# Where the early work of a fused backward kernel is placed: transposes, late tables and weight-gradient pieces in the first eight steps

## The chip, the cores and the metric

The kernel runs on one core of one Trainium2 chip. The metric is the device time of one execution in microseconds (us), the median of several runs. The core has a matrix engine (TensorE, "PE" in the profile), a vector engine (VectorE, "DVE"), a scalar engine for activations and copies (ScalarE, "ACT"), a general engine (GpSimd, "POOL") and a queue that only issues transfers (SyncE, "SP"). Each works through its own list of instructions, and they meet through semaphores. Matmul results land in PSUM, [...]from which ACT or DVE must copy them before the bank can be used again.

## The reference

A gate mixes two branches, and the kernel returns the mixture and the gradients of all inputs but one:

```python
g = sigmoid((x * gate_w).sum(-1, keepdims=True))
a = irfft2(rfft2(x) * (w_r + 1j * w_i))           # over 2048 x 576
b = (gelu(x @ w_gate) * (x @ w_up)) @ w_down      # 576 -> 4608 -> 576
out = g * a + (1 - g) * b
# and, for grad_out: the gradients of x, w_r, w_i, w_gate, w_up, w_down, gate_w
```

x and grad_out are 2048 x 576 in bf16. In the kernel the Fourier transforms are matmuls with tables of sines and cosines.

## The kernel before

**Tiling.** The 2048 rows are 16 tiles of 128. The 4608 hidden columns are worked on in 18 groups g of 256 (`NG`, `FG`). A group has four steps m, each over four row tiles, so there are 72 steps, numbered pr = 4g + m. A second phase after the 72 steps multiplies stored results with the weights; the change does not touch it.

**A step.** `H_mm` (L378) lists the matmuls: z, the gradient dOT against w_down (L388, L391), and xy, the gate and up products (L395, L402), into two PSUM tiles, called the first and second half here. `H_da` (L409) copies z out on ACT, scaled by 1-g. `H_act` (L415) copies one half of xy out on ACT: part 0 is the square q (L419), part 1 is the plain copies xb and hu (L421, L422). `H_ew1` (L424) is three DVE instructions on q and xb. `H_ew2` (L440) is two sigmoids on ACT (L443, L444) and eight DVE products (L448 to L455), the last of them dHg. Of the working tiles q, s and om there is one buffer each, of xb and hu two. So q of a step cannot be written before the product om (L450) of the step before has read the old q.

**The weight gradients.** `W_units` (L468) lists matmuls over the A, dHu, dHg of one group: four units w (L505), one tail unit (L518), and four units d (L488), which multiply A with the gradient tile dB. They run one group later: those of group 0 in steps 4 to 7, with a rest carried into step 8. Each is evacuated by ACT (L466) and stored by POOL's queue.

**The transforms.** `fft` is a list of some 200 small units, and `want(pr)` says how many are to be done by step pr. In the first steps they are u1 (six matmuls L562, a copy Y on ACT, L567) and u2 (two matmuls L579, a copy ve on ACT, L583, two DVE instructions, a store). `pftile` (L541) gives them their PSUM tile: in group 0 two tiles in turn, named pg and z, and from group 1 on only z, which the step's own z product also uses. The first unit of a step is put between the matmuls of the second half of xy (`between`, L399).

**Other early work.** `titems` (L347) transposes four row tiles in three pieces: matmuls with the identity (L355, L358), then a copy on DVE or ACT (L359). `build_R` (L141) makes four tables: five DVE instructions, and a sine on ACT that is put off until `run_late` (L106). `columns_B` (L158) and `build_B` (L192) make another table in the same way, on DVE and POOL, with a sine in `run_late`. `scale_dB` (L940) multiplies tiles of dB by 1-g on DVE, in place; units d need all 16 scaled, the transposes need them unscaled.

The order on every engine is that in which the Python program calls the instructions; there is no planner that reorders.

Of the kernel before, what the change touches and what calls it, by code (L numbers as in the profile page):

```python
# [20 lines left out]
P, T = 128, 16  # L21
# [207 lines left out]
def kernel(  # L229
# [4 lines left out]
    nc = tc.nc  # L234
# [64 lines left out]
    tb = iotas(nc, res, unit)  # L299
# [109 lines left out]
    def H_da(m, z):  # L409
        da = ewt("da")  # L410
        for t in range(4):
            nc.scalar.activation(da[:, t, :], z[:, t % 2, t // 2, :], ACT.Copy, scale=omg32[:, 4 * m + t:4 * m + t + 1])  # L412
        return da

    def H_act(k, xy, tiles, part):  # L415
        xb, q, hu = tiles
        h = slice(2 * k, 2 * k + 2)
        if part == 0:
            nc.scalar.activation(q[:, h, :], xy[:, :, 0:FG], ACT.Square)  # L419
        else:  # L420
            nc.scalar.copy(xb[:, h, :], xy[:, :, 0:FG])  # L421
            nc.scalar.copy(hu[:, h, :], xy[:, :, FG:2 * FG])  # L422

    def H_ew1(tiles):  # L424
        xb, q, hu = tiles
        s = ewt("s")
        V.tensor_scalar(s[:], q[:], A_GELU, 1.0, op0=ALU.mult, op1=ALU.add)
        V.tensor_tensor(s[:], xb[:], s[:], op=ALU.mult)
        V.tensor_scalar(q[:], q[:], 6.0 * A_GELU * C_GELU, 2.0 * C_GELU, op0=ALU.mult, op1=ALU.add)
        return s  # L430
# [37 lines left out]
    def W_units(g):  # L468
        fsl = slice(g * FG, (g + 1) * FG)
        kt = kept[g]  # L470

        def tl(k, t):
            return kt[t // 4][k][:, t % 4, :]
        dwd_tiles, wp = {}, {}

        def halves(f, us):
            return [(us, lambda: f(0)), (us, lambda: f(1))]

        def wtile(key):
            if key not in wp:  # L480
                wp[key] = pw.tile([P, TPB, FG], F32, tag="wps", name="wps")
            return wp[key]

        def u_dwd(fch, h):
            def f(half):
                wps = wtile(("d", fch, h)).rearrange("p a b -> p (a b)")
                for t in range(8 * half, 8 * half + 8):
                    nc.tensor.matmul(wps[:, :288], lhsT=tl(0, t)[:, fch * P:(fch + 1) * P],  # L488
                                     rhs=dB[:, t, h * 288:(h + 1) * 288], start=(t == 0), stop=(t == T - 1))
                if half == 0:  # L490
                    return
                if h == 0:
                    dwd_tiles[fch] = stage.tile([P, D], BF16, tag="dwd", name="dwd")
                dwd = dwd_tiles[fch]
                wevac(dwd[:, h * 288:(h + 1) * 288], wps[:, :288])
                if h == 1:
                    r0 = g * FG + fch * P
                    wst[0].dma_start(out_6[r0:r0 + P, :], dwd[:])
            return halves(f, 1.0)

        def u_dw(k, ov, c0):
            def f(cc):
                wps = wtile(("w", k, c0))
                for t in range(T):
                    nc.tensor.matmul(wps[:, cc, :], lhsT=xn[:, t, (c0 + cc) * P:(c0 + cc + 1) * P],  # L505
                                     rhs=tl(k, t), start=(t == 0), stop=(t == T - 1))
                if cc == 0:
                    return
                dw = stage.tile([P, TPB, FG], BF16, tag="dw", name="dw")
                wevac(dw[:], wps[:])  # L510
                wst[0].dma_start(ov[:, c0:c0 + TPB, fsl], dw[:])  # L511
            return halves(f, 1.7)

        def tail(half):
            wps = wtile("t")
            for t in range(8 * half, 8 * half + 8):
                for k, r in ((1, LO), (2, HI)):
                    nc.tensor.matmul(wps[r, 0, :], lhsT=xn[:, t, 512:576], rhs=tl(k, t),  # L518
                                     start=(t == 0), stop=(t == T - 1))
            if half == 0:  # L520
                return
            dw = stage.tile([P, FG], BF16, tag="dwt", name="dwt")
            wevac(dw[:], wps[:, 0, :])
            wst[0].dma_start(out_4[512:576, fsl], dw[LO, :])
            wst[0].dma_start(out_5[512:576, fsl], dw[HI, :])
        tl_ = halves(tail, 1.0)
        w = [u_dw(k, ov, c0) for k, ov in ((1, o4v), (2, o5v)) for c0 in range(0, 4, TPB)]
        d = [u_dwd(fch, h) for fch in range(FCH) for h in range(2)]
        if g == 0:
            return [[w[0], tl_], d, [w[1]], [w[2]], w[3]]  # L530
        return [[d[0]], [d[1], d[2], d[3]], [w[0], tl_], [w[1], w[2]], w[3]]


# [347 lines left out]
    build_R(nc, tb, unit, 0)  # L881
    build_R(nc, tb, unit, 4)
    run_late(tb)
    columns_B(nc, tb, res)
    makeB = build_B(nc, tb, unit, res)

    fg = zipped(*fwd_units(xT, scr_x, None)) + zipped(*fwd_units(dOT, scr_g, gs32))
# [17 lines left out]
    mid_at = 4 * T + 10  # L905
    NPR = NT // 2
    LASTP = NG * NPR - 7
    FIRST = (0, 0, 1, 3)
    done = [0]

    def want(pr):

        n0 = FIRST[-1]
        if pr < NPR:
            return FIRST[pr]

        def load(n):

            return n + 0.5 * min(max(n - mid_at, 0), n_mid)
        share = load(n0) + (load(n_slots) - load(n0)) * (pr + 1 - NPR) / (LASTP - NPR)  # L920
        n = n0
        while n < n_slots and load(n + 1) <= share + 1e-9:
            n += 1
        return int(min(n, n_slots) + 1e-9)
# [20 lines left out]
    for g in range(NG):  # L945
        if g == 1:
            pgs.close()
            pw = ps1.enter_context(tc.tile_pool(name="pw", bufs=2, space=PSUM, **kw))
        for m in range(NPR):
            pr = g * NPR + m  # L950
            n = want(pr) - done[0]
            done[0] += n
            hs = [h for u in pend[m] for h in u] if pend else []

            def side_work(us):
                while side and us > 0:
                    us -= side[0][0]
                    side.pop(0)[1]()
            z, xy_full = H_mm(g, m)
            tiles = [ewt(tag) for tag in ("xb", "q", "hu")]  # L960
            xy = xy_full(0)
            da = H_da(m, z)
            H_act(0, xy, tiles, 0)
            flush()
            H_act(0, xy, tiles, 1)
            state = []
            titem = titems(dB, dOT, 4 * m + 8, pgtile, (VC, VC, AC)) if g == 0 and m < 2 else []
            if titem:
                titem.pop(0)()

            def second():
                xy = xy_full(1, titem.pop(0) if titem else fft_next if n else None)
                for part in range(2):
                    H_act(1, xy, tiles, part)
                state.append(H_ew1(tiles))
                side_work(4.4)

            def sigs():
                H_ew2(g, m, tiles, state[0], da)
            if g == 0:  # L980
                second()
                for f in titem:
                    f()
                for _ in range(n - 1):
                    fft_next()
                sigs()
                if m == 0:
                    next(makeB)
                elif m < 3:
                    build_R(nc, tb, unit, 4 * m + 4)  # L990
                else:
                    next(makeB)
            else:
                second()
                at, k = 0.0, min(n, 1)
                spots = (0.0, 1.6, 3.6) if n < 4 else (0.0, 1.0, 2.6, 4.2, 5.0, 5.0)
                for w, f in carry + hs:
                    if k < n and at >= spots[k]:
                        fft_next()
                        k += 1  # L1000
                    if pr == NG * NPR - 1 and at == 0.0:
                        sigs()
                    f()
                    at += w
                while k < n:
                    fft_next()
                    k += 1
                if pr == NPR:
                    run_late(tb)
                if pr < NG * NPR - 1:  # L1010
                    sigs()
            carry = []
            flush(len(stores) - 1)
            if m < 3 and g + 1 < NG:
                load_w(g + 1, m)
            if (g, m) in ((0, 3), (1, 0)):
                scale_dB(T // 2)
            if done[0] == n_slots or (pr >= wgT_from and pr % 2 == 0 and len(wgT_all) < 20):
                load_wgT()
                if done[0] == n_slots:  # L1020
                    load_wgT()
        carry = pend[4] if pend else []
        pend = W_units(g)
# [241 lines left out]
```

## Time and profile before

| what | value |
|---|---|
| median of three runs | 1427.95 us (1427.85 to 1428.72) |
| the profiled execution | 1427.79 us |
| its span in the profile | 1426.0 us |
| busy PE / DVE / ACT / POOL | 1389.1 / 730.4 / 727.0 / 124.5 us |
| chain that ended last, by engine | PE 92%, DVE 3%, ACT 3%, issue 1% |
| PE busy from 20 to 130 us | 90.4 of 110 us |
| PE busy from 130 to 300 us | 170 of 170 us |

The span is the time from the first to the last instruction of the profile; the execution's own time is 1.8 us more. A busy PE is counted from modelled ends of pipelined matmuls, so short gaps can hide in it. All times in the text are counted from the start of the span.

### The profile page before, as it was taken

Reading aid. Unit: us, or ns where it says so; the run is one execution under the profiler, and the core shown is the slowest. Engines: PE = TensorE matmul, PEld = TensorE weight load, DVE = VectorE, ACT = ScalarE, POOL = GpSimd, SP = SyncE. Lnnn points to the kernel's source line nnn. Section 1 sums busy time; section 2 is a strip of 40 time slices with the busy share of each in tenths; the row PEclk is TensorE's granted clock in tenths of the full one; section 3 lists DMA queues with packets and bytes.
Section 4 is the critical chain, followed back from the end, with each engine's and each line's share of the span. In section 5 each row is a group of like instructions: output and inputs, shape, how many; then the busy total and the mean of one; then the engine's idle time right before and its main releaser. Section 6 shows DMA issues by size and latency. Waiting matters only on the chain.

```text
span 1426.0 us, 28214 instructions
## 1 busy us (share of the span) xinstructions
PE 1389.1 (97%) x11431; PEld 1022.3 (72%) x11431; DVE 730.4 (51%) x1395; ACT 727.0 (51%) x1321; POOL 124.5 (9%) x226
## 2 busy tenths in 40 slices
PE   7789999999999999999999999999999999999997
PEld 5456767676667767767777777768777777777776
DVE  6765656555988877775656566551000642212100
ACT  7667777768878788776777777662000000000000
POOL 3000000110101101110010100110000100000000
PEclk9999999999999999999999999999999999999999
DMA  5333433444546655555455564759999998778773
GB/s 179 96 99 113 129 113 109 120 138 124 145 134 171 163 137 149 150 146 141 118 159 157 137 165 128 170 126 248 211 195 203 224 191 168 163 153 168 155 150 77
DMA packets 514655, 214.63 MB, mean 151 GB/s; under 512 B 311418, under 2 KB 508732, under 8 KB 514524
## 3 DMA queue, kind: packets, MB, share of 16 engines
q1 hardware_dynamic: 504988, 192.32, 56.9%
q0 software_dynamic: 7728, 19.49, 4.2%
q8 instruction: 89, 1.46, 0.4%
q10 hardware_dynamic: 1808, 1.02, 0.3%
q14 instruction: 42, 0.34, 0.1%
HBM read 41.05 MB, written 93.84 MB: 95 GB/s over the span
## 4 chain that ended last, share of the span: by engine, by line
PE 92%; DVE 3%; ACT 3%; issue 1%; DMA 0%; POOL 0%; SPq 0%; POOLq 0%; DVEq 0%; ACTq 0%
PE acc L1110 29%; PE wps L505 17%; PE xy L402 16%; PE wps L488 10%; PE z L388 8%; PE wps L518 2%; PE xy L395 2%; PE pf L562 2%; PE z L391 1%; PE pf L833 1%; PE pf L761 1%; PE pf L835 1%; PE pf L672 1%; PE pf L579 0%; ACT s L444 0%
## 5 line engine op out<-in xcount | busy, mean ns | idle before, releaser
L1110 PEld LDWEIGHTS <-pin 128*128 128x128 bf16 x3456 | 338.0, 98 | 85.3 <-issue 0.2
L402 PE MATMUL xy<-wgu,xT 128*128 128x512 bf16 x1152 | 271.7, 380 | 0.0
L505 PEld LDWEIGHTS <-xn 128*128 128x128 bf16 x2304 | 224.9, 98 | 39.4 <-issue 1.2
L402 PEld LDWEIGHTS <-xT 128*128 128x128 bf16 x1152 | 106.0, 98 | 136.9 <-issue 30.9
L1127 ACT COPY bo<-acc 128x288 f32<-128x288 f32 x32 | 12.8, 400 | 305.0 <-PE acc L1110 305.0
L448 DVE TENSOR_TENSOR xb<-xb,s 128x1024 bf16<-128x1024 bf16 x72 | 49.9, 692 | 223.0 <-ACT s L444 222.8
L488 PE MATMUL wps<-dB,A 128*128 128x288 bf16 x1152 | 154.5, 286 | 0.3 <-DVE dB L942 0.3
L1110 PE MATMUL acc<-wgT,pin 128*128 128x288 bf16 x1152 | 143.8, 286 | 0.0
L1110 PE MATMUL acc<-wuT,pin 128*128 128x288 bf16 x1152 | 143.6, 286 | 0.0
L1110 PE MATMUL acc<-wd_all,pin 128*128 128x288 bf16 x1152 | 142.6, 286 | 0.0
L388 PE MATMUL z<-wdT,dOT 128*128 128x256 bf16 x1152 | 137.8, 273 | 3.9 <-ACT Y L567 2.4
L505 PE MATMUL wps<-dHg,xn 128*128 128x256 bf16 x1152 | 136.7, 273 | 0.8 <-DVE dHg L455 0.8
L488 PEld LDWEIGHTS <-A 128*128 128x128 bf16 x1152 | 112.2, 98 | 32.6 <-issue 1.8
L505 PE MATMUL wps<-dHu,xn 128*128 128x256 bf16 x1152 | 135.5, 273 | 0.0
L388 PEld LDWEIGHTS <-dOT 128*128 128x128 bf16 x1152 | 111.2, 98 | 22.4 <-issue 8.4
L419 ACT ACTIVATE q<-xy 128x512 bf16<-128x512 f32 x144 | 87.8, 610 | 63.2 <-DVE om L450 56.5
L412 ACT ACTIVATE da<-z,omg 128x256 bf16<-128x256 f32 x288 | 111.8, 470 | 0.6 <-PE z L391 0.6
L1187 DVE SCALAR_TENSOR_TENSOR f32t<-gwf,dlog,b16t 128x576 f32<-128x576 f32 x16 | 13.1, 817 | 172.5 <-DMA b16t<-dxa_scr 172.5
L511 POOL DMA_DIRECT2D out_dram<-dw x67 | 49.2, 734 | 581.1 <-ACT dw L466 576.4
L422 ACT CAST hu<-xy 128x512 bf16<-128x512 f32 x144 | 89.0, 618 | 0.0
L421 ACT CAST xb<-xy 128x512 bf16<-128x512 f32 x144 | 85.6, 595 | 0.0
L466 ACT CAST dw<-wps 128x512 bf16<-128x512 f32 x72 | 42.2, 586 | 78.0 <-PE wps L505 77.7
(207 smaller groups left out, 1596.6 us busy)
## 6 DMA issues: line engine op xcount, KB each, us to landing
scr<-A SPq DMA_DIRECT2D x72, 256.0 KB, 2.4
scr<-dHg SPq DMA_DIRECT2D x72, 256.0 KB, 2.7
scr<-dHu SPq DMA_DIRECT2D x72, 256.0 KB, 3.0
out_dram<-dw POOLq DMA_DIRECT2D x67, 128.0 KB, 3.0
wd_all<-in_B_w_down_dram SPq DMA_DIRECT2D x3, 1728.0 KB, 14.4
out_dram<-dwd POOLq DMA_DIRECT2D x34, 144.0 KB, 3.3
scr_p<-Vt SPq DMA_DIRECT2D x32, 145.0 KB, 3.4
wgu<-in_B_w_gate_dram SPq DMA_DIRECT2D x18, 256.0 KB, 3.6
```

Source lines behind the costliest of these rows:

```text
L388: nc.tensor.matmul(zo(t), lhsT=dOT[:, ci, t, :], rhs=wdT[:, ci, :], start=(t % 4 < 2 and ci == 0), stop=False)
L402: nc.tensor.matmul(xy[k][:, t % 2, :], lhsT=xT[:, ci, t, :], rhs=wgu[:, ci, :], start=False, stop=(ci == 3))
L412: nc.scalar.activation(da[:, t, :], z[:, t % 2, t // 2, :], ACT.Copy, scale=omg32[:, 4 * m + t:4 * m + t + 1])
L419: nc.scalar.activation(q[:, h, :], xy[:, :, 0:FG], ACT.Square)
L421: nc.scalar.copy(xb[:, h, :], xy[:, :, 0:FG])
L422: nc.scalar.copy(hu[:, h, :], xy[:, :, FG:2 * FG])
L448: V.tensor_tensor(xb[:], xb[:], s[:], op=ALU.mult)
L466: nc.scalar.copy(out, in_)
L488: nc.tensor.matmul(wps[:, :288], lhsT=tl(0, t)[:, fch * P:(fch + 1) * P], rhs=dB[:, t, h * 288:(h + 1) * 288], start=(t == 0), stop=(t == ...
L505: nc.tensor.matmul(wps[:, cc, :], lhsT=xn[:, t, (c0 + cc) * P:(c0 + cc + 1) * P], rhs=tl(k, t), start=(t == 0), stop=(t == T - 1))
L511: wst[0].dma_start(ov[:, c0:c0 + TPB, fsl], dw[:])
L1110: nc.tensor.matmul(acc[:, :288], lhsT=src[:, r, :], rhs=w_of(r)[:, h * 288:(h + 1) * 288], start=(first and r == 0), stop=(last and r == F ...
```

## The change

The three pieces of transposes for row tiles 12 to 15 of the gradient move from step 1 to step 0; those of tiles 8 to 11 stay in step 0. All but the first two of the six pieces now stand ahead of `H_ew1` of that step. In every step the copies of the first half of xy come in the order xb, hu, q in place of q, xb, hu. `columns_B` moves from the head of the kernel to step 5, the two parts of `build_B` from steps 0 and 3 to steps 5 and 6, `build_R` for tables 8 to 11 and 12 to 15 from steps 1 and 2 to steps 5 and 6, and `run_late` for all of these from step 4 to step 6. All 16 tiles of dB are scaled in step 4, between `H_ew1` and `H_ew2`; before, eight were scaled at the end of step 3 and eight at the end of step 4. Of the pieces of group 0's weight gradients, step 5 has three d units and step 6 one d and one w unit; before, step 5 had four d and step 6 one w. The count of transform units by the end of steps 4 to 7 is written out as 6, 10, 14, 17; `want` gave 6, 10, 14, 18 before.

```diff
         if g == 0:
-            return [[w[0], tl_], d, [w[1]], [w[2]], w[3]]
+            return [[w[0], tl_], d[:3], [d[3], w[1]], [w[2]], w[3]]
...
     run_late(tb)
-    columns_B(nc, tb, res)
     makeB = build_B(nc, tb, unit, res)
...
-    FIRST = (0, 0, 1, 3)
+    FIRST = (0, 0, 1, 3, 6, 10, 14, 17)
...
         n0 = FIRST[-1]
-        if pr < NPR:
+        if pr < len(FIRST):
             return FIRST[pr]
...
-        share = load(n0) + (load(n_slots) - load(n0)) * (pr + 1 - NPR) / (LASTP - NPR)
+        share = load(n0) + (load(n_slots) - load(n0)) * (pr + 1 - len(FIRST)) / (LASTP - len(FIRST))
...
             da = H_da(m, z)
+            H_act(0, xy, tiles, 1)
             H_act(0, xy, tiles, 0)
             flush()
-            H_act(0, xy, tiles, 1)
             state = []
-            titem = titems(dB, dOT, 4 * m + 8, pgtile, (VC, VC, AC)) if g == 0 and m < 2 else []
-            if titem:
+            titem = []
+            if pr == 0:
+                titem = titems(dB, dOT, 8, pgtile, (VC, VC, AC)) + titems(dB, dOT, 12, pftile, (VC, VC, AC))
                 titem.pop(0)()
 
             def second():
                 xy = xy_full(1, titem.pop(0) if titem else fft_next if n else None)
                 for part in range(2):
                     H_act(1, xy, tiles, part)
+                while titem:
+                    titem.pop(0)()
                 state.append(H_ew1(tiles))
+                if pr == 4:
+                    scale_dB(T)
+                elif pr == 5:
+                    columns_B(nc, tb, res)
+                    next(makeB)
+                    build_R(nc, tb, unit, 8)
+                elif pr == 6:
+                    next(makeB)
+                    build_R(nc, tb, unit, 12)
                 side_work(4.4)
...
             if g == 0:
                 second()
-                for f in titem:
-                    f()
                 for _ in range(n - 1):
                     fft_next()
                 sigs()
-                if m == 0:
-                    next(makeB)
-                elif m < 3:
-                    build_R(nc, tb, unit, 4 * m + 4)
-                else:
-                    next(makeB)
             else:
...
-                if pr == NPR:
+                if pr == 6:
                     run_late(tb)
...
-            if (g, m) in ((0, 3), (1, 0)):
-                scale_dB(T // 2)
```

## The prediction

> **What bounds the kernel now.** I read three things in order. First the page's busy times by slice: the matrix engine is full everywhere except in the first four slices of 35.65 us.
>
> ```profile
> PE   7789999999999999999999999999999999999997
> DVE  6765656555988877775656566551000642212100
> ```
>
> So a change to the first eight steps can gain only what PE idles there, 19.6 us between 20 and 130 us (90.4 busy of 110); from 130 to 300 us PE is busy 170 of 170. Second, PE's waits between 20 and 170 us, line by line with the releaser:
>
> ```profile
> PE pf L355 <- DVE dOT L359: 5.6, 1, 5.6
> PE pf L562 <- ACT da L412: 4.5, 2, 2.7
> PE pf L579 <- ACT da L412: 3.1, 1, 3.1
> PE pf L562 <- ACT ve L583: 2.6, 3, 1.0
> PE z L388 <- ACT Y L567: 2.4, 3, 0.9
> ```
>
> All of them lie in the stretch concerned. Third, the timeline says what released them. On DVE in steps 1 and 2:
>
> ```profile
> 50.20 0.69 DVE L455 TENSOR_TENSOR dHg<-hu,om 128x1024 bf16<-128x1024 bf16 x1
> 50.80 1.13 DVE L148 SCALAR_TENSOR_TENSOR XR<-kk,scol 128x128 int32<-128x128 f32 x4
> 51.97 0.43 DVE L149 TENSOR_SCALAR XR<-XR 128x512 int32<-128x512 int32 x1
> 52.32 0.42 DVE L427 TENSOR_SCALAR s<-q 128x1024 bf16<-128x1024 bf16 x1
> ...
> 53.56 1.06 ACT L443 ACTIVATE om<-s 128x1024 bf16<-128x1024 bf16 x1 [2.13 <-DVE s L428]
> ```
>
> In group 0 the bound is a loop of ACT and DVE, not PE: two sigmoids (om to the start of DVE's L448, 2.21), eight products (5.19 to the next start), then L427 and L428 (1.24 until om). That is 8.64 us; the table instructions (50.80 to 52.32) make it 10.14, and the sigmoids of steps 1, 2, 3 start at 43.40, 53.56, 63.70. From step 4 the bound passes to PE, with two more losses on the way: the late sines, and the scaling of dB.
>
> ```profile
> 77.07 1.28 ACT L154 ACT_TABLE_LOAD   x1
> 78.37 1.33 ACT L154 ACTIVATE Rt<-XR,pi 128x512 bf16<-128x512 int32 x2
> 79.61 0.49 ACT L222 ACTIVATE oB<-XBi,pi 128x256 f32<-128x256 int32 x1
> 80.12 1.28 ACT L443 ACT_TABLE_LOAD   x1
> 81.41 1.06 ACT L443 ACTIVATE om<-s 128x1024 bf16<-128x1024 bf16 x1
> ```
>
> And on PE, in the next step:
>
> ```profile
> 85.06 0.41 PE L579 MATMUL pf<-Y,Rt 128*128 128x290 bf16 x2 [3.12 <-ACT da L412]
> ```
>
> ACT is busy without a break from 77.07; da comes behind the sigmoids, and the transform unit between the xy matmuls needs the z bank that da empties.
>
> **The Trainium skill.** PSUM — Partial Sum Buffer, "Engine vs sequencer instructions", says that the queues of ScalarE, VectorE and GpSimd are strictly first in, first out. The trace agrees: ACT's q waits 0.81 us in step after step for om (L450) while the ready xb stands behind it. ScalarE: Activation LUTs, "What ACT_TABLE_LOAD costs", gives 1.28 us for a load and 2.66 with a drain. Here the load is 1.28 and the next activation starts 1.30 after it, so I use 1.3. TensorE: Matmul & The Clock Gate, "What's actually happening", says that the array falls to half clock after an idle window of about 3.4 us. The trace agrees: PE idles 5.62 us up to 38.73, and the granted clock from 36 to 42 us is 0.50.
>
> **Part 1, step 0.** Three pieces (24 transposes, three copies) join step 0, and DVE and ACT do their copies ahead of the chain. All run through few PSUM tiles. ACT copies the third piece from 28.64 to 29.3, as now. Piece 4 takes pg: transposes from 29.35, copy on DVE 0.65 later, to 30.7. Piece 5 takes the z tile, copied by 31.3. Piece 6 needs pg again: transposed at 30.75, copied by ACT from 31.3 to 31.8. Only then the table load (29.33 now), so the sigmoid om of step 0 starts at 33.1 in place of 30.62: 2.5 late. DVE has L428 ready at 32.5, so it isn't last. In return step 1 has no transposes. PE's 5.62 us wait at 38.73, the matmuls at half clock behind it and ACT's 4.89 us idle before q at 41.48 go, and om of step 1 starts one loop later, 33.1 + 8.64 = 41.75 (43.40 now): 1.65 early.
>
> **Part 2, the loop.** Without `build_R` steps 2 and 3 come at 50.4 and 59.05 (53.56 and 63.70). ACT is not next in line: sigmoids 2.15, da 1.46, three copies twice 2.9, Y 0.53, ve 0.55 are 7.6 under 8.64. The order xb, hu, q takes the 0.81 wait away because da and two copies (2.4) outlast it, but here DVE ends last, so I credit nothing. In all later steps PE is the bound; nothing too. The last dHg of group 0 ends at 59.05 + 2.2 + 5.28 = 66.5, now 71.15. The w matmuls waiting for it start 4.66 early. **First term: 4.66.**
>
> **Part 3, step 4.** `run_late` is gone here. PE ends its tail at 66.55 + 5.36 = 71.9, dwt is copied by 72.4, then om, s (2.15) and da (1.46) by 76.0. PE arrives at the unit between at 66.55 + 10.73 = 77.3, so the 3.12 wait is gone. **Second term: 3.12.** The 16 scalings of dB at 0.279 (73.0 to 75.2 for eight) are 4.46 on DVE from 68.05 to 72.5, a ve pair (0.75) behind them, and `H_ew2` of step 4 can't start before 74.6. So they cost nothing, with 1.3 us of cover; if that is short, da's q and step 5 are late by the excess.
>
> **Part 4, steps 5 to 7.** From 86.17 to the z matmul at 125.28 PE takes 39.1 us. Counted by starts, the work is 32.7: 64 L488 at 0.1225 (7.84), six u1 at 0.75 and five u2 at 0.25 (5.75), two steps' z and xy (6.07 each), 64 L505 at 0.109 (7.0). So 6.4 are lost. They are the 0.67 for ve, 1.5 in which L488 waits for and is paced by the scaling of dB (88.78 to 91.1), and four waits of 0.73 to 0.97 where two units follow each other on the one z tile, as steps 6 and 7 have four units and only two w pieces between which to put them. After: dB is long scaled; the pieces 6, 4, 2 leave one unit at the end of step 6 and one of step 7, each paid by the next z, which waits for the copy behind dw: 0.7 and 1.05. `run_late` moves to the end of step 6: 1.3 + 1.33 + 0.4 + 1.28 = 4.3 of ACT ahead of om. There da would be 1.6 ahead of PE's arrival (next z starts 1.45 after the last w, then 5.2 of matmuls; da ends at 1.4 + 2.2 + 1.46), so 2.7 show. Losses after: 4.45. **Third term: 6.4 - 4.45 = 1.95.**
>
> Hidden: `columns_B` and tables 8 to 11 (1.2 + 1.5 on DVE in step 5) and `build_B`, tables 12 to 15 (1.95 + 1.5 in step 6) stand between `H_ew1` and `H_ew2`, where DVE now idles 6.56 and 4.6 us. Without that cover they would delay the sines. POOL's 6.0 us (25.07 to 31.07) come after step 4's stores and before step 5's dwd stores; two dwd tiles are enough until step 8. SP gets no transfer more; the Vt stores move with their units, and the w_down loads for group 1 are issued behind step 1's stores, 2 us earlier. One unit fewer by step 7 is made up later, when PE is the bound: 0.75 owed, not gained (in 32.7 it is counted on both sides).
>
> **Sum:** 4.66 + 3.12 + 1.95 = 9.7. The profiled execution took 1427.79 (span 1426.0 and 1.8 around it), 0.16 under the median of the runs: 1427.8 - 9.7 = **1418.1 us**.
>
> **Unknown.** The tables' working tiles and Y, ve come from one pool of 18 buffers, and the trace shows no buffer numbers. In steps 5 and 6 four transform units per step now run while six or seven table tiles are held, where before there was at most one or two. If Y of step 6 gets a buffer that `build_B` has just left, ACT waits for DVE until some 4 us later: between 0 and 6 us in all. I take 0, since none of the waits of before is of this kind, also in the middle part. The new order of the copies may also save part of the 3 us that PE idles from 300 to 900: 0 to 2. `run_late` may show 0 (if ACT has idled) to 4.3. These make 1414.5 to 1424.
>
> **Rivals.** (a) The forecast, 1414.5 to 1420.5: 0.68. (b) Buffers or DVE's crowding in steps 4 to 6 cost 4 to 6 us: 1422 to 1424. For it, DVE gets 10.6 us of extra work in three steps; against it, idle time of that size is there. 0.15. (c) The bound doesn't move: step 0's delay and the sines at step 6 eat what the loop gives, for example if `run_late` shows all 4.3 and step 0 is 5 late. Against it: the loop alone is 3 us shorter by step 3. 1425.2 to 1430.8: 0.05. (d) Slower: q last in all 72 steps makes each step's chain later than PE can bear. A loss of 0.14 us per step takes back the 9.7; at 0.2 us the time is 1427.8 - 9.7 + 14.4 = 1432.5. For it, only that q heads the DVE chain; against it, q's wait ends at the same om (L450) either way and xy's second half is untouched. With unnamed harm of the same sign, 0.12. That the change doesn't do what it says I exclude: each moved call is unconditional for its step.
>
> **How the numbers follow.** The point is case a's. The range 1414.5 to 1424 holds a and b, 0.83. A measurement of this kernel can tell about 0.2%, 2.9 us: faster is a and b, 0.83; the same is c, 0.05; slower is d, 0.12.
>
> **What would show it.** Right: no PE wait near 38; sigmoids of steps 1 to 3 some 8.65 apart, starting near 41.8, 50.4, 59.0; the L505 wait near 66.5; no wait for da in step 5; one of 2 to 3 us for da in step 7, behind two table loads; ACT's q no longer waiting for om. Wrong: table loads that start well after 32; ACT's Y or ve waiting for DVE in steps 5 and 6; dB or its scaling as a releaser; a PE that waits in small pieces after 130 us.

## The result, and the profile after

The changed kernel takes 1486.57 us (median of 4 runs, 1484.52 to 1487.6), the kernel before 1428.34 (1427.85 to 1429.4): a ratio of 1.0405, 95% interval 1.0387 to 1.0423. The forecast of 1418.1 us promised 9.7 us less; the kernel takes 58 us more. The profiled execution of the changed kernel takes 1484.52 us with a span of 1482.7.

First the page's busy times by slice (a slice is now 37.07 us):

```profile
PE   7899999999768988699999999999999999999997
DVE  5876565558557756577556655655000561212110
PEclk9999999999889999899999999999999999999999
```

The head is fuller than before, but PE now has holes in slices 11 to 17, some 370 to 630 us, a part in which the change touches only the order of three copies and the count of transform units. The waits of PE over the whole span (total, times, longest):

```profile
PE z L388 <- ACT Vt L764: 53.4, 7, 12.5
PE z L388 <- ACT ve L583: 3.1, 2, 2.1
...
PE pf L562 <- ACT da L412: 2.6, 1, 2.6
PE pf L579 <- ACT da L412: 2.6, 1, 2.6
PE pf L355 <- ACT dOT L359: 2.2, 1, 2.2
```

One row, 53.4 us, is nearly as large as the whole loss of 58 us. Two tables follow: the first eight steps, where the forecast looked, and the way from there to the end.

| event, us from the start | before | forecast | after |
|---|---|---|---|
| sigmoid om of step 0 starts | 30.62 | 33.1 | 33.12 |
| of step 1 | 43.40 | 41.75 | 41.73 |
| of step 2 | 53.56 | 50.4 | 50.36 |
| of step 3 | 63.70 | 59.05 | 58.98 |
| unit between in step 5 | 85.06 | 77.3 | 77.06 |
| PE's wait for da in step 7 | none | 2.7 | 2.59 |
| z of step 8 (first matmul) | 125.28 | 114.8 | 114.86 |

| step (start of its L391 matmuls, us) | before | after | difference |
|---|---|---|---|
| 9 | 140.78 | 129.96 | -10.8 |
| 26 | 371.92 | 362.09 | -9.8 |
| 27 | 384.85 | 384.89 | 0.0 |
| 30 | 423.50 | 438.77 | +15.3 |
| 33 | 462.14 | 486.47 | +24.3 |
| 36 | 500.62 | 532.45 | +31.8 |
| 39 | 538.15 | 578.83 | +40.7 |
| 42 | 576.73 | 630.93 | +54.2 |
| 45 | 615.47 | 671.12 | +55.65 |

A gain of the forecast's size is there until step 26. Then six jumps, one every third step, and a small one in step 45 take back 65.5 us. The timeline of DVE has the loop without its table instructions:

```profile
48.50 0.69 DVE L455 TENSOR_TENSOR dHg<-hu,om 128x1024 bf16<-128x1024 bf16 x1
49.11 0.42 DVE L427 TENSOR_SCALAR s<-q 128x1024 bf16<-128x1024 bf16 x1
```

and PE's has the unit of step 5 without a wait:

```profile
77.06 0.41 PE L579 MATMUL pf<-Y,Rt 128*128 128x290 bf16 x2
```

**What happens in a jump.** The stretch is the middle of the transform list. A pair p of row tiles has units s2 (L672) and then four units m0, m1, n0, n1 (`s1` in the code, L761); the eight pairs are counted from 0. Each of the four copies its result on ACT into a tile Vt, of which there are two, and SP stores it (L766). Unit m1 first calls `prefetch(p + 2)`, 14 loads, and only then issues its own store. SP in step 26 of the changed kernel:

```profile
368.66 0.50 SPq L459 DMA_DIRECT2D scr<-dHu  x1
369.21 0.54 SPq L637 DMA_DIRECT2D Vp<-scr_x  x1
369.79 0.74 SPq L637 DMA_DIRECT2D Vp<-scr_g  x1
370.64 3.62 SPq L663 DMA_DIRECT2D Wt<-in_A_w_r_dram  x6
374.38 3.56 SPq L663 DMA_DIRECT2D Wt<-in_A_w_i_dram  x6
378.04 3.69 SPq L766 DMA_DIRECT2D scr_p<-Vt  x3
```

ACT's three copies in the same step:

```profile
366.23 0.84 ACT L764 CAST Vt<-pf 128x580 bf16<-128x580 f32 x1
...
368.76 0.82 ACT L764 CAST Vt<-pf 128x580 bf16<-128x580 f32 x1 [0.25 <-PE pf L761]
...
380.53 0.81 ACT L764 CAST Vt<-pf 128x580 bf16<-128x580 f32 x1 [9.44 <-DMA scr_p<-Vt]
```

And PE's next z:

```profile
381.39 3.57 PE L388 MATMUL z<-wdT,dOT 128*128 128x256 bf16 x16 [8.58 <-ACT Vt L764]
```

The three copies are m1, n0 and n1. The first is done at 367.1, but SP issues the loads from 369.21 to 377.9 and the store of m1 only at 378.04. (The row of three stores holds m1's, n0's and, from 381.37, n1's own.) n1 needs m1's tile; it waits until that store has landed, and holds the bank of the z tile (its piece of PSUM) meanwhile, so PE waits 8.58 us for the bank. Then the array runs at half clock for a while: behind the six long waits the granted clock is 0.50 or 0.51 for 3.0 to 6.0 us, 26.7 us in all. Half of that, 13 us, is an estimate of what this adds; it is close to the 12 us by which the 65.5 us of delay exceed the 53.4 us of waits.

The small delay in step 45 belongs to pair 6. Its m1, n0 and n1 share a step too, but its m1 has no loads to issue (`p + 2 < T // 2` is false), and PE waits 0.93 us there in place of 5.6 to 12.5.

In the kernel before, m0 and m1 of a pair fall into one step, n0 and n1 into the next. SP's store of m1 at the same pair:

```profile
375.77 0.39 SPq L766 DMA_DIRECT2D scr_p<-Vt  x1
```

and ACT's copy of n1:

```profile
378.59 0.83 ACT L764 CAST Vt<-pf 128x580 bf16<-128x580 f32 x1
```

There the loads are issued from 368.22 to 375.7 us, ahead of n0's copy and not behind it. m1's store goes out at 375.77 and takes 2.7 us to land, and n1 comes at 378.59, 2.8 us after it was issued: in time by 0.1 us. The changed kernel does one unit fewer by step 7 and spreads the rest by a formula that starts there, and m1 falls behind the border of a step: m0 | m1 n0 n1 in place of m0 m1 | n0 n1. By the two traces this is so for pairs 0 to 6, and pair 7 is as before. That was a reading of two profiles; the runs test it as a cause.

### The profile page after: what moved, and what is told of

Its sections match the earlier page's. It is cut to its first block, busy times and chain, and to the rows that moved or that the text cites. A ratio compares the mean times of both kernels' runs of the same rounds, so it can differ in the third digit from the quotient of the medians.

```text
span 1482.7 us, 28153 instructions
## 1 busy us (share of the span) xinstructions
PE 1400.7 (94%) x11431; PEld 1026.1 (69%) x11431; DVE 730.1 (49%) x1395; ACT 730.9 (49%) x1321; POOL 124.7 (8%) x226
## 4 chain that ended last, share of the span: by engine, by line
PE 84%; DVE 5%; ACT 4%; DMA 3%; SPq 3%; issue 1%; POOL 0%; ACTq 0%; DVEq 0%; POOLq 0%
PE acc L1111 28%; PE wps L505 15%; PE xy L402 15%; PE wps L488 8%; PE z L388 8%; PE xy L395 2%; PE wps L518 2%; PE pf L562 1%; PE z L391 1%; DMA Vp<-scr_g 1%; SPq L663 1%; DMA scr_p<-Vt 1%; ACT s L444 1%; ACT om L443 1%; PE pf L833 1%
## 5 line engine op out<-in xcount | busy, mean ns | idle before, releaser
L505 PEld LDWEIGHTS <-xn 128*128 128x128 bf16 x2304 | 224.6, 98 | 39.0 <-issue 0.6
L388 PE MATMUL z<-wdT,dOT 128*128 128x256 bf16 x1152 | 148.0, 285 | 58.6 <-ACT Vt L764 53.4
L388 PEld LDWEIGHTS <-dOT 128*128 128x128 bf16 x1152 | 115.9, 102 | 83.0 <-issue 64.0
L505 PE MATMUL wps<-dHg,xn 128*128 128x256 bf16 x1152 | 136.5, 273 | 0.2 <-DVE dHg L455 0.2
L505 PE MATMUL wps<-dHu,xn 128*128 128x256 bf16 x1152 | 135.7, 273 | 0.0
L421 ACT CAST xb<-xy 128x512 bf16<-128x512 f32 x144 | 85.2, 592 | 33.1 <-PE xy L402 33.1
```

Source lines behind the costliest of these rows:

```text
L388: nc.tensor.matmul(zo(t), lhsT=dOT[:, ci, t, :], rhs=wdT[:, ci, :], start=(t % 4 < 2 and ci == 0), stop=False)
```

## The experiments

Theory COUNT says that the count of units, the written number 17 with the formula behind it, is all of the loss. Theory EARLY says that the moved work is, through other buffers or a fuller ACT. All ratios are to the kernel before on the same chip, whose median there is 1429.4 to 1431.5 us; in the result above it was 1428.3, so times are not subtracted across the two.

**The change without its count.** The kernel e1 keeps every move and takes back the count:

```diff
-    FIRST = (0, 0, 1, 3, 6, 10, 14, 17)
+    FIRST = (0, 0, 1, 3)
-        if pr < len(FIRST):
+        if pr < NPR:
-        share = ... (pr + 1 - len(FIRST)) / (LASTP - len(FIRST))
+        share = ... (pr + 1 - NPR) / (LASTP - NPR)
```

> The changed kernel with the old count of transform units (18 by step 7, and the old formula for all later steps); all moved work stays moved. Theory COUNT (one unit fewer by step 7 shifts the middle part, so that the pieces m1, n0, n1 of a pair fall into one step, and the third of them waits for a Vt buffer whose store stands behind 14 loads in SP's queue): 1417 us, 1414 to 1420, no wait of Vt for a store over 2 us, PE's waits for Vt below 2 us in all. Rival EARLY (the moved tables and the new order of the copies take other buffers or crowd ACT, and the count is innocent): about 1486 us, with the 53 us of waits for Vt still there.

Measured: 1421.87 us against 1431.45, ratio 0.994 (0.9925 to 0.9955). By the medians 9.6 us are gained (6.4 to 10.7 by the interval), where the forecast had 9.7; the time itself lies above the 1414 to 1420 us expected, on a chip where the kernel before takes 3 us more. All eight pairs are m0 m1 | n0 n1 again, no wait of PE for Vt is listed, and ACT's three waits for a store of Vt are 3.2 us in all. EARLY falls.

**The count without the change.** The reverse edit in the kernel before.

> The kernel before with the new count of transform units alone. COUNT: six jumps of 8 to 14 us between steps 26 and 42 as in the changed kernel, 65 us in all, so 1428 + 65 = 1493 us, 1483 to 1500. EARLY: 1428 us, within 3.

Measured: 1496.48 us, ratio 1.0455 (1.044 to 1.0471), 65.0 us more by the medians. PE's waits:

```profile
PE z L388 <- ACT Vt L764: 54.2, 7, 12.3
```

Its pairs fall into steps as in the changed kernel. So the count is enough, without any of the moved work.

**A third Vt tile.** The changed kernel with one link of the chain taken out:

```diff
-tc.tile_pool(name="half", bufs=2, side="right")
+tc.tile_pool(name="half", bufs=3, side="right")
-            dw = stage.tile([P, FG], BF16, tag="dwt", name="dwt")
+            dw = stage.tile([P, FG], BF16, tag="dw", name="dwt")
```

> The changed kernel with three buffers for Vt in place of two (room for it comes from letting the tail's store tile share the two tiles of the w pieces). COUNT with the buffer as the link: the third Vt has a buffer at once, PE's waits for Vt fall below 5 us, 1415 to 1422 us. Rival LOADS (SP is simply late with everything in the middle, the buffer only shows it): PE waits for Vp or ACT for stores in place of it, at least half of the 65 us stays, over 1445 us.

Measured: 1426.91 us (1424.23 to 1429.99), ratio 0.9968 (0.9957 to 0.9979): 5.0 us over e1 on the same chip, so all but 5 of the 65 us are gone, though the time is above the range expected. ACT waits for no Vt store in the middle any more. SP is late with the same stores as without the edit (the three go out from 380.64, behind the same 14 loads), and no engine is seen waiting for them. What is left comes between the L391 matmuls of steps 27 and 28, and it is a different wait: PE for a piece of w_down that SP issues late, 3.1 us in two waits at 389 to 393 us.

**The store ahead of the loads.** The other link, with two Vt tiles:

```diff
-                if key == "m1" and b == 1 and p + 2 < T // 2:
-                    prefetch(p + 2)
...
                 LD.dma_start(dst[g:g + 2].rearrange("g q l -> q g l"), Vt[:])
+                if key == "m1" and b == 1 and p + 2 < T // 2:
+                    prefetch(p + 2)
```

> The changed kernel with the loads of the pair after next issued behind the store of the same unit's Vt and not ahead of it; two buffers as they were. COUNT with SP's order as the link: the store that the third Vt waits for is issued at once, and only 1415 to 1422 us are left. LOADS: the loads take the same time in SP's queue, the next stores wait behind them, over 1445 us.

Measured: 1446.24 us, ratio 1.0102 (1.0087 to 1.0117): 24.4 us over e1 stay and some 40 of the 65 are gone, between the two expectations. SP says why, here for pair 1 (the copy of m1 is done at 411.1):

```profile
404.60 6.41 SPq L741 DMA_DIRECT2D out_dram<-o  x12
411.11 0.64 SPq L282 DMA_DIRECT2D wgu<-in_B_w_gate_dram  x1
...
416.97 1.13 SPq L764 DMA_DIRECT2D scr_p<-Vt  x1
```

The loads no longer stand ahead of the store, but 12 stores of o, the weight loads of the next group and the step's own stores do. SP is issuing without a break from 404.6 until that store is out; n1 waits 6.6 us, PE 5.7. So the 14 loads are the larger part of what delays these stores, not all of it. The Trainium skill has a case like this in Perfetto Trace Analysis, "What 'DMA-bound' means": the track of the issuing engine is solid with slices, and what such a slice measures is the making of descriptors, not the movement. The trace of the changed kernel agrees in part. From 369.2 to 378.0 us SP issues but for one gap:

```profile
SPq L663 <- DMA Vp<-scr_g: 1.0, 1, 1.0
```

The 16 transfer engines are busy 0.99 of the time from 369.2 to 374 us and 0.24 from 374 to 378. A load of Wt occupies SP for 0.42 us in the median in both parts, so most of the delay is issuing; the gap, and one load that takes SP 1.15 us while the engines are full, can be due to the movement.

**The change whole, the middle realigned.** One empty place moves from the start of the middle to its end; the count stays 17.

```diff
-        out = [first] + [gap] * 7
+        out = [first] + [gap] * 6
...
- ... mid[-2:] + [gap] * 2 + ia[:-4] ...
+ ... mid[-2:] + [gap] * 3 + ia[:-4] ...
```

> The changed kernel whole, with its own count of 17, but one empty place in the list of units moved from the start of the middle part to its end (6 and 3 in place of 7 and 2), so that the pieces of a pair fall into steps as in the kernel before: m0, m1 in one step, n0, n1 in the next. COUNT: all of the 65 us go though nothing early is undone, ratio to before 0.993 to 0.995 (1420 to 1424 us on a chip where before takes 1431). Rival: if 17 by step 7 itself hurts (later waits, buffers), over 1440 us.

Measured: 1421.59 us against 1429.44, ratio 0.9948 (0.9934 to 0.9963). In pairs 0 to 6 the pieces stand m0 m1 | n0 n1 again. It isn't the number 17 as such but where the pieces of a pair fall.

**A dose.** With 18 as the last number and the new formula behind it, only the pairs 4, 5 and 6 have m1, n0, n1 in one step.

> The changed kernel with 18 in place of 17 as the last written number and the new formula after it. By the list, only the pairs 4, 5 and 6 then have m1, n0, n1 in one step; in the changed kernel's profile these three jumps are 8.8, 13.8 and 1.3 us. COUNT: about 24 us over e1, ratio to before about 1.011 (1440 to 1452 us), and PE waits three times for Vt, all after step 37. Rival (the count of 17 is the cause by itself and not where the pieces fall): as e1, ratio 0.994.

Measured: 1442.79 us, ratio 1.0094 (1.0079 to 1.0109), some 22 us over e1 by the ratios. So the formula alone, which starts four steps later than before, already moves three pairs; the number 17 moves the other four. Its three waits, from PE's timeline, are the three that were named, in steps 38, 41 and 44:

```profile
536.43 3.23 PE L388 MATMUL z<-wdT,dOT 128*128 128x256 bf16 x16 [6.80 <-ACT Vt L764]
585.01 3.57 PE L388 MATMUL z<-wdT,dOT 128*128 128x256 bf16 x16 [8.60 <-ACT Vt L764]
627.37 1.91 PE L388 MATMUL z<-wdT,dOT 128*128 128x256 bf16 x16 [0.94 <-ACT Vt L764]
```

**The parts of the gain.** Five kernels take one part each out of e1, to test the terms of the sum.

The transposes back (step 1 again has three pieces, and what is left of them comes after the chain):

```diff
-            titem = []
-            if pr == 0:
-                titem = titems(dB, dOT, 8, ...) + titems(dB, dOT, 12, ...)
+            titem = titems(dB, dOT, 4 * m + 8, pgtile, (VC, VC, AC)) if g == 0 and m < 2 else []
+            if titem:
...
-                while titem:
-                    titem.pop(0)()
...
                 second()
+                for f in titem:
+                    f()
```

> e1 (the change with the old count) with the transposes of row tiles 12 to 15 back in step 1 and behind the chain. By the prediction's sum their move is worth 1.65 us (sigmoid of step 1 at 43.4 in place of 41.75): 1.7 us over e1, ratio about 0.995. Rival, that the 5.6 us wait of PE at 38 us is worth its full size: 5 us over e1.

The tables and their sines back:

```diff
+    columns_B(nc, tb, res)
     makeB = build_B(nc, tb, unit, res)
...
-                elif pr == 5:
-                    columns_B(nc, tb, res)
-                    next(makeB)
-                    build_R(nc, tb, unit, 8)
-                elif pr == 6:
-                    next(makeB)
-                    build_R(nc, tb, unit, 12)
...
+                if m == 0:
+                    next(makeB)
+                elif m < 3:
+                    build_R(nc, tb, unit, 4 * m + 4)
+                else:
+                    next(makeB)
...
-                if pr == 6:
+                if pr == NPR:
                     run_late(tb)
```

> e1 with the tables of the second half and their sines back at their old places (head, steps 0 to 3, sines at the end of step 4). By the sum: 1.5 us in each of steps 2 and 3, a wait of 3 us for da in step 5 in place of one of 2.6 in step 7: 3.3 us over e1, ratio about 0.9965. Rival, that the sines cost the same anywhere and the loop has slack: within 1 us of e1.

The scaling of dB back:

```diff
-                if pr == 4:
-                    scale_dB(T)
...
+            if (g, m) in ((0, 3), (1, 0)):
+                scale_dB(T // 2)
```

> e1 with the scaling of dB back in two halves (end of step 3, end of step 4). By the sum the second half comes too late for the first d pieces and PE is paced by DVE: 1.5 us over e1, ratio about 0.995. Rival, hidden: as e1, 0.994.

The deal of the pieces back:

```diff
-            return [[w[0], tl_], d[:3], [d[3], w[1]], [w[2]], w[3]]
+            return [[w[0], tl_], d, [w[1]], [w[2]], w[3]]
```

> e1 with the old deal of the w pieces (four d in step 5, one w in step 6). By the sum, step 6 gets back two waits of 0.73 to 0.97 where units follow each other on the z tile, in place of one of 0.73: 1.0 us over e1. Rival: the pieces only change places, as e1.

The order of the copies back:

```diff
-            H_act(0, xy, tiles, 1)
             H_act(0, xy, tiles, 0)
             flush()
+            H_act(0, xy, tiles, 1)
```

> e1 with the old order of the copies (q first). By the sum 0: ACT's wait of 0.81 us for om in every step comes back, and the time stays that of e1 within 1 us. Rival (the order saves what PE idles from 300 to 900 us, about 3 us): 3 us over e1. Rival (the order harms by 0.14 us in 71 steps): 10 us under e1.

| e1 without | ratio to before (95%) | over e1, from the ratios' medians | expected |
|---|---|---|---|
| (e1 itself) | 0.9940 (0.9925 to 0.9955) | | |
| the transposes | 0.9954 (0.9938 to 0.9971) | 2.0 us | 1.65 |
| the tables | 0.9973 (0.9963 to 0.9983) | 4.7 us | 3.3 |
| the scaling of dB | 0.9950 (0.9937 to 0.9962) | 1.4 us | 1.5 |
| the deal | 0.9959 (0.9946 to 0.9971) | 2.7 us | 1.0 |
| the order of the copies | 0.9968 (0.9956 to 0.9980) | 4.0 us | 0 |

The third column is the difference of the two ratios times 1430 us; each ratio is uncertain by 1.4 to 2.4 us, so only the tables and the order of the copies stand clear of e1, and no single row contradicts its term but the last. The rest is compatible with the terms and doesn't prove them. The rows add up to 14.8 us, more than e1's whole gain; the parts overlap, so they needn't agree. For the last row the trace shows a place: with q first, PE's z of step 4 waits 3.42 us for ve and starts at 60.40; in e1 it waits 2.20 and starts at 58.74. By the starts of the steps in the two profiled executions, e1 is 1.7 us ahead at step 7 and 2.2 at step 71, so at most 0.5 us of it can come from the stretch of 300 to 900 us that the rival named. How the 4.0 us of the medians come about isn't settled: in some executions the array falls to half clock behind one of these waits of 2 to 3 us, in others it doesn't. In e1's profiled execution 16 L505 matmuls take 3.35 us by starts at 111.26, where the changed kernel takes 1.75, and that execution took 1425.44 us where the other three took 1421.3 to 1422.1. A part of each row can be this chance and not the part that was taken out.

## Why the prediction was wrong

**The view of what bounds the kernel** held for the head and was closed too soon. "A change to the first eight steps can gain only what PE idles there" is true of a gain. It says nothing of what the steps hand on. They hand on a position in a list, and from step 8 each unit's place follows from it.

**The step that failed** stands at the end of the paragraph "Hidden": "One unit fewer by step 7 is made up later, when PE is the bound: 0.75 owed, not gained". It took the units for interchangeable PE work. They aren't: in the middle each of a pair's last four units has a copy, a tile and a transfer in SP's queue, and where they fall against a step decides whether a store gets out before its tile is needed. It also took the change for one of a single unit, where the formula for all later steps moved with it. "SP gets no transfer more" was true by count and missed what counts, which transfer stands ahead of which. This term cost about 65 us, not 0.75: 65.5 by the starts of the steps, 65.0 in e2, which has it alone; in e1 and f1 the loss is absent.

**The sentence on the unknown** named a buffer that is still held as the danger, in another pool, and set it to 0 because "none of the waits of before is of this kind, also in the middle part". Of the kind it meant, a copy that waits for DVE to leave a buffer, that is true. But ACT's waits in the kernel before, from 330 to 700 us, have the kind that mattered:

```profile
ACT Vt L764 <- DMA scr_p<-Vt: 3.6, 4, 1.5
```

Four times a Vt copy already waited for the store of its tile. It is small, and no wait of PE for Vt is listed, so no cost is seen; but it says that this link had little slack left.

**The terms of the head** were right to a few tenths, as the first table shows: 4.66 for the loop (4.7 measured at the sigmoid of step 3), 3.12 for da in step 5 (the wait is gone), 2.7 for the sines at their new place (2.59). z of step 8 came at 114.86 against 114.8 forecast, and e1 measures the sum, 9.6 against 9.7. That these agree to a tenth is partly luck. The losses that part 4 names for the kernel before add up to 5.6 us, not to its 6.4. The count alone brings z of step 8 from 125.28 to 123.62 (e2), 1.7 us where the forecast had 0.75, and 1.0 of it is given back by step 21. And e1's interval is 6.4 to 10.7 us; f1, with all of the early moves, gains 7.9 by the medians.

**The rivals.** (b) was the right kind of mechanism with the wrong buffers, the wrong steps and a tenth of the size. (d), slower by q last in each step, is refuted: with q first e1 isn't faster but slower, and e1's lead over the kernel before in the profiles stays between 5.1 and 5.3 us from step 8 to step 71, so no loss builds up over the steps. (c) is refuted by e1. The predicted signs of no wait for da in step 5, of one of 2 to 3 us in step 7 and of no PE wait near 38 all came true, which shows that signs which all lie in the head can't confirm an end-to-end time.

**"I credit nothing" for the order of the copies** may be too little: p5, e1 with q first, is 4.0 us over e1 by the ratios, with about 2 us of uncertainty on each. The forecast compared ACT's and DVE's loop only, and had not asked when ve leaves the z tile for PE in step 4.

## What to carry to other kernels

When work is dealt from one list into steps, a changed count can shift all that follows: write the list against the steps for the whole run, before and after, and look for units that now share a step, not only at those that moved. For each tile with few buffers, find its store in the issuing queue and count what stands ahead of it; a small wait of a copy for a store of the tile it needs is a sign that this link has little slack. If a prefetch of many small loads and a store of a scarce tile share a queue, try one more buffer for the tile: here, at the bad alignment, that left 5.0 us of the 65, and putting the store first left 24.4. The early moves themselves are sound: with the count taken back, or with one empty place moved, the changed kernel is 0.5 to 0.6% faster than the kernel before.

## What the runs showed of the hardware

Twelve small loads of Wt keep SP's queue from 370.64 to 377.94 us in the changed kernel, 0.42 us each in the median, while the transfer engines are busy 0.99 of the time up to 374 us and 0.24 from 374 to 378: much of what holds up the store behind them is issuing.

Behind the six waits of 5.6 to 12.5 us in the changed kernel the 16 z matmuls take 3.34 to 3.57 us; behind the wait of 0.93 us they take 1.91. Waits of 2 to 3 us didn't act alike on PE's clock. In e1's profiled execution it fell to 0.50 behind the wait of 2.59 us in step 7; in the changed kernel it was 1.00 from 108 to 114 us, behind a wait of the same length. A wait of 2.60 us that ended at 45.39 in the changed kernel was followed by 0.51 from 46 to 49 us, and one of 3.12 us that ended at 85.06 in the kernel before by 1.00 from 80 to 90. So the prediction's window of about 3.4 us is no safe bound below which the clock holds.
